# Three tile groups of an attention and two-layer kernel placed 64 bytes further on, and attention's conversions begun in other groups

## The chip, the cores and the metric

The kernel runs on one core of one Trainium2 chip. The metric is the device time of one execution in microseconds (us). Before the change the median of three executions is 1054.4 us (1048.92 to 1058.47).

## What is computed

```python
def _attn_ref(q, k, v):                       # q, k, v: (4, 12, 448, 64)
    S = q.shape[2]
    scores = np.matmul(q, k.transpose(0, 1, 3, 2)) / np.sqrt(64) - np.log(S)
    return np.matmul(1.0 / (1.0 + np.exp(-scores)), v)

def _moe_ref(x, w_in, w_out):                 # x: (1792, 768), w_in: (768, 2048), w_out: (2048, 768)
    h = x @ w_in
    return (h / (1.0 + np.exp(-h))) @ w_out

def _moe2_ref(x, w_in, w_out, a, b):          # the same sizes
    h = x @ w_in
    P = a[0] + a[1]*h + a[2]*h**2 + a[3]*h**3
    Q = 1.0 + abs(b[0])*abs(h) + abs(b[1])*h**2
    return (P / (Q + 1e-06)) @ w_out

# out = _moe2_ref(_moe_ref(heads of _attn_ref side by side, ...), ...)
```

The weights arrive as 64-bit floats and are cut to 32-bit ones on the chip.

## The kernel before, in words

**Three stages, one order.** The program fixes the order of the work by hand: each engine runs its instructions in the order in which they stand in the code. A wait on an engine holds up all that stands behind it there. Attention (L1009 to L1120) comes first, then layer 1 (its first product with `w_in1` in 16 groups by Strassen's seven products, its second with `w_out1` behind it), then layer 2.

**Operands in two parts.** For more precision each matmul operand is split into a high part (a copy on ACT) and a low part (a subtraction on DVE). A product is then three matmuls: high by high, high weights by low x, low weights by high x. Layer 1's first product (`product`, L540 to L552) issues 16 groups x 7 products x 9 = 1008 matmuls of 448 columns. Its weights are the parts `wr` and `wq`; its moving side is x in the tiles `xb` and `xa_all`. Layer 1's second product (`second`, L687 to L697) streams parts in `xa_all` against weights `woH`, `woL`. Layer 2's first product (`first2`, L756 to L772) streams x parts that lie either in the six `hx` tiles or in `xa_all`, against `woH`, `woL`, with 512 or 384 columns. The weight parts of index 0 and 1 lie in the four tiles `w0` (the profile calls them `w`).

**Attention.** The 24 pairs of heads are worked two at a time: an even pair e and an odd one o = e+1. One round of e has three groups (`quads`, L1036 to L1047). Below they are called A, B and C:

- A: steps n = 2e and 2e+1; units (e,0), (e,1), (e,2); no new pair.
- B: step 2e+2; units (o,0), (o,1); prepares pair e+2.
- C: step 2e+3; units (o,2) and (e,3), the second of which is shared by both pairs; prepares pair e+3.

A unit is `attn_QK` on PE (L351, k's parts as weights, q's parts moving, 448 columns, two halves of the array side by side), then a sigmoid on ACT (`attn_S`, L366), and one group later `attn_AV` on PE (L375). Three PSUM tiles `pair` go round. A unit takes one until its sigmoid has read it; a prepared pair's transposed k (`attn_T`, L323) takes one until the copy on ACT (L334) and the subtraction on DVE (L336) have read it. `attn_E` (L388, L391) empties `hb` on DVE in group A, before the next `attn_AV` of that round may write it. `attn_X` (L328) transposes q on DVE. From e = 6 on, each group also begins a split of layer 1's x (L408 on ACT, L413 on DVE, some subtractions L450 on POOL).

**Conversions.** `conv` (L194) cuts a 128x768 slab of 64-bit weights. It is an `Abs` on ACT that waits for the slab's load (L203), two cheap DVE operations (L204, L205), and the `rest`: two DVE operations (L208, L211). In attention it is begun at the end of the group that holds step n, if n is in `CONVS`; the rest runs in the following group, behind that group's `attn_C` (or behind `attn_E` in A); and `conv_outs` at the start of the group after that sends the result away on the SP queue (L177) and asks for the next slab (`conv_load`, L161 and L163). The first two slabs are asked for at n = 0 and n = 3. Twelve conversions are begun in attention, the others in the layers.

**Where the tiles lie.** Offsets within a partition follow from the sizes of the tiles. The left pools begin with `sb`, `ident` and five small tiles, so `xa_all` begins 32 bytes behind a multiple of 128; `xb`, `wr`, `wq` and `woH2` to `woL15` all are whole multiples of 128 behind it, and so do they. k's parts (`kst`) and two of q's three buffers (`qst`) lie in `xa_all`, also at 32. The right pools end at a fixed address; `hx`, `w0` and q's third buffer `qx` begin 96 bytes behind a multiple of 128. The slices that the matmuls take out of the tiles begin whole multiples of 128 into them.

Of the kernel before, what the change touches and what calls it, by code (L numbers as in the profile page):

```python
# [11 lines left out]
F32 = mybir.dt.float32  # L12
# [29 lines left out]
def attention_moe_moe(ctx: ExitStack, tc: tile.TileContext, q, k, v, w_in1, w_out1, w_in2, w_out2, a, b2, out):  # L42
    nc = tc.nc
    B, H, S, D = q.shape
    NT, DM = out.shape
    DFF = w_out1.shape[0]
    P = 128
# [9 lines left out]
    BK = 512  # L57
    ONE = 1.0 + 1e-6
    QKSCALE = 1.0 / math.sqrt(D)
    NEG_LOG_S = -math.log(S)  # L60
    NST = 2

    cpool = ctx.enter_context(tc.tile_pool(name="cpool", bufs=1))
    dr_p = ctx.enter_context(tc.tile_pool(name="dr", bufs=1, space=DRAM))

    def fixed(nm, n, shape, dt, pool=cpool):
        return [pool.tile(shape, dt, tag=f"{nm}{i}", name=f"{nm}{i}") for i in range(n)]

    def opened(name, side=None, space=None):
        stack = ExitStack()  # L70
        kw = {"space": space} if space is not None else {}
        if side is not None:
            kw["side"] = side
        pool = stack.enter_context(tc.tile_pool(name=name, bufs=1, reuse_waits="tile", **kw))
        ctx.push(stack)
        return pool, stack

    REST_SB = DM - S
    sizes = (10 * S, 3 * BK, *(2 * DM,) * NST, *(DM,) * 2, REST_SB)
    sb = cpool.tile([P, sum(sizes)], F32, tag="sb", name="sb")  # L80
    sb_at = [sum(sizes[:i]) for i in range(len(sizes) + 1)]
# [6 lines left out]
    xio = Ring([x_all[:, i, :] for i in range(3)])  # L88
    stage = Ring([t.bitcast(I32).rearrange("p (e t) -> p e t", t=2) for t in sb_[2 : 2 + NST]])
    bits = Ring(sb_[2 + NST : 4 + NST])  # L90
    xs = [[dr_p.tile([P, NT], F32, tag=f"xs{m}_{d}", name=f"xs{m}_{d}") for d in range(KD)] for m in range(2)]
# [79 lines left out]
    def conv_outs():  # L171
        for do in outs:
            do()
        outs.clear()
# [64 lines left out]
    ld_p = [None]  # L239
# [18 lines left out]
    def load_k(i):  # L258
        if i < NPT:
            ks[i] = ks_t[i % 4]  # L260
            load_by_key(k, ks[i], i, nc.scalar if i < 2 else nc.sync)

    def load_q(i):
        if i >= NPT:
            return
        b, hp = divmod(i, NP)
        t = qs[i] = ld_p[0].tile([P, S], F32, tag="qs", name=f"qs_{i}", bufs=3)
        for part in range(2 * D // SQ):
            j, e0 = divmod(part * SQ, D)
            (nc.scalar if i == 0 and part % 2 else nc.sync).dma_start(  # L270
                out=t[part * SQ : (part + 1) * SQ, :].rearrange("l (c d) -> l c d", d=SQ),
                in_=q[b, 2 * hp + j, :, e0 : e0 + SQ].rearrange("(c l) d -> l c d", l=SQ),
            )
# [3 lines left out]
    def mix(i):  # L277
        if i >= NPT:
            return
        t = ks.pop(i)  # L280
        u = mixed[i] = ld_p[0].tile([P, 2 * NCH * D], F32, tag="km", name=f"km_{i}", bufs=2)
        (nc.gpsimd if i else nc.vector).tensor_copy(
            u.rearrange("p (c h d) -> p h c d", c=NCH, h=2), t.rearrange("p h (c d) -> p h c d", c=NCH)
        )
# [8 lines left out]
    xa_all = xa_p.tile([P, 9 * 2 * S], F32R, tag="xa_all", name="xa_all")  # L293
# [6 lines left out]
    xk_p, xk_s = opened("xk")  # L300
    xk = fixed("xk", 2 * KD, [P, S], F32, xk_p)
    wr, wq = [], []
    K3 = 3 * 2 * BK
    kst = Ring([xa_all[:, i * 2 * BK : (i + 1) * 2 * BK].rearrange("p (j s) -> p j s", j=2) for i in range(3)])
    qst = Ring([xa_all[:, K3 + i * 2 * S : K3 + (i + 1) * 2 * S].rearrange("p (j s) -> p j s", j=2) for i in range(2)])

    hb = []
    st, at = {}, {}
# [17 lines left out]
    def attn_X(i):  # L326
        x = xq[i] = ld_p[0].tile([P, S], F32, tag="xq", name=f"xq_{i}", bufs=1)
        nc.vector.transpose(x, qs.pop(i))  # L328
# [35 lines left out]
    def attn_S(i, c, p):  # L364
        t = f2.get()
        nc.scalar.activation(t, p[:, :, :S], AF.Sigmoid, bias=nls, scale=QKSCALE)  # L366
        pairs.put(p)
        at[i, c] = t
# [42 lines left out]
    def flush():  # L411
        for src, h, lo in lows:
            nc.vector.tensor_tensor(out=lo, in0=src, in1=h.bitcast(F32), op=ALU.subtract)  # L413
        lows.clear()
# [37 lines left out]
    def operands0():  # L452
        X, W, Y, Z = (xk[n_ * HK : (n_ + 1) * HK] for n_ in range(4))
        for kk in range(HK):
            split_p(X[kk], 0, "11", kk)
            yield
            split_p(W[kk], 0, "21", kk)
            if kk == HK - 1:
                sub_p(X[0], Y[0], X[0])
            yield  # L460
        for kk in range(HK):
            x, w, y, z = X[kk], W[kk], Y[kk], Z[kk]
            split_p(x, 0, "T1", kk)
            sub_p(y, z, y)
            yield
            split_p(y, 0, "T3", kk)
            yield
            split_p(z, 0, "22", kk)
            sub_p(y, z, x)
            yield  # L470
            split_p(y, 0, "T2", kk)
            sub_p(w, w, y)
            if kk + 1 < HK:
                sub_p(X[kk + 1], Y[kk + 1], X[kk + 1])
            yield
            split_p(w, 0, "T4", kk)
            yield
# [525 lines left out]
    with tc.manual_schedule():  # L1003
# [7 lines left out]
        pairs.put(*fixed("pair", 3, [P, 2, 512], F32, ps_p))  # L1011
        ks_t.extend(fixed("ks", 4, [P, 2, NCH * D], F32, ld_p[0]))
        qst.put(ld_p[0].tile([P, 2, S], F32R, tag="qx", name="qx"))
        for i in range(2):
            load_k(i)
            load_q(i)
# [14 lines left out]
        load_q(3)  # L1031
        load_k(4)
        first_ops = operands0()
        CONVS = (3, 6, 10, 14, 18, 22, 26, 29, 33, 36, 39, 42)
        waiting = []
        def quads():  # L1036
            for e in range(0, NPT, 2):
                o, n = e + 1, 2 * e
                if e == 0:
                    yield e, (0,), [(e, 0), (e, 1)], 1  # L1040
                    yield e, (1,), [(e, 2)], 2
                    yield e, (2,), [(o, 0), (o, 1)], NPT
                    yield e, (3,), [(o, 2), (e, LAST)], 3
                else:
                    yield e, (n, n + 1), [(e, 0), (e, 1), (e, 2)], NPT
                    yield e, (n + 2,), [(o, 0), (o, 1)], e + 2
                    yield e, (n + 3,), [(o, 2), (e, LAST)], e + 3  # L1047

        for e, steps, units, new in quads():
            conv_outs()  # L1050
            flush()
            if 0 in steps:
                mix(2)
            for n in steps:
                if n % 2:
                    mix(n // 2 + 3)
            if new < NPT:
                attn_X(new)
            ready = [(u, attn_QK(*u)) for u in units]
            p = attn_T(new) if new < NPT else None  # L1060
            for u, p_ in ready:
                attn_S(*u, p_)
            for u in waiting:
                attn_AV(*u)
            waiting = units
            if steps[0] == 2 * e and e:
                attn_E(e - 2)
                attn_E(e - 1)
            if p is not None:
                attn_C(new, *p)  # L1070
            if new < NPT:
                load_q(new + 3)
            conv_rest()
            if e >= NP:
                next(first_ops, None)
            for n in steps:
                i, h = divmod(n, 2)
                if h == 0:
                    load_k(i + 5)
                at_half = n - 2 * NPT  # L1080
                if n % 4 == 1:
                    load_v(e + 2)
                    load_v(e + 3)
                if at_half == -8:
                    load_w1(0)
                    load_w1(1)
                if at_half == -5:
                    xk_s.close()
                    wr_p, wr_s = opened("wr")
                    wr.extend(fixed("wr", 4, [P, DM], F32R, wr_p))  # L1090
                    wq.extend(fixed("wq", 6, [P, HM], F32R, wr_p))
                    prep_ij(0)
                    sums_12(0)
                if at_half == -3:
                    prep_s12(0)
                if at_half == -1:
                    prep_a22(0)
                if n == 0:
                    conv_load()
                if n == 3:  # L1100
                    conv_load()
                if n == 4:
                    coefficients()
                if n == 12:
                    coefficients_abs()
                if n in CONVS:
                    conv(True)
# [8 lines left out]
        ps_s.close()  # L1116
        w0_p = ctx.enter_context(tc.tile_pool(name="w0", bufs=1, side="right", reuse_waits="tile"))
        w0 = fixed("w0", 4, [P, DM], F32R, w0_p)
        woH.extend(w0[0::2])
        woL.extend(w0[1::2])  # L1120
        kt_p, kt_s = opened("kt", side="right")
# [233 lines left out]
        for n in range(HN):  # L1355
            g, p = turn(n)
# [31 lines left out]
            if n > 3 * HF:  # L1388
                i = n - 3 * HF - 1
# [85 lines left out]
```

## Time and profile before

| | us |
|---|---|
| executions: median (lowest, highest) | 1054.4 (1048.92, 1058.47) |
| the profiled execution | 1053.23 |
| its span, first to last instruction | 1051.4 |
| PE busy | 1036.2 (99% of the span) |
| DVE, ACT, POOL busy | 773.3, 605.8, 263.8 |
| attention, until layer 1's first matmul | about 167.8 |

The time is that of the whole execution; the span is what the profile sees of it, 1.8 us less. PE counts as busy while any matmul is on its way, and matmuls overlap, so 99% doesn't mean that each streams at its best rate: the distance from one matmul's start to the next one's is what counts.

### The profile page before, as it was taken

What the parts mean: (1) busy time and instruction counts of PE and PEld (TensorE: products, weight loads), DVE (VectorE), ACT (ScalarE), POOL (GpSimd) and SP (SyncE); (2) the same over time, 40 slices, a digit from 0 to 9 for tenths busy, and PEclk for the clock granted to TensorE, in tenths of its full rate; (3) what the DMA queues carried; (4) which work ended last, traced back from release to release, by engine and by line L of the source; (5) the groups of instructions that cost most, each with busy time, mean ns of one, the idle gap of its engine ahead of it and who ended that gap; (6) DMA issues with size and microseconds to landing.
All of it is one profiled execution on the core that took longest, in us unless ns stands there. A gap on an engine that the chain in (4) does not pass through costs nothing.

```text
span 1051.4 us, 15990 instructions
## 1 busy us (share of the span) xinstructions
PE 1036.2 (99%) x5558; PEld 895.7 (85%) x5558; DVE 773.3 (74%) x1104; ACT 605.8 (58%) x911; POOL 263.8 (25%) x233
## 2 busy tenths in 40 slices
PE   8999999999999999999999999999999999999998
PEld 5555457999998988899998888888999999999998
DVE  3678885888978758686877847879898977545761
ACT  4788785556655545433343458666777857354430
POOL 4235520000000000000000046769868931300000
PEclk9999999999999999999999999999999999999999
DMA  9989895777558765799899844657678878876641
GB/s 172 234 196 202 226 263 198 264 257 244 187 200 287 253 234 201 241 316 320 295 338 351 319 166 135 236 177 233 240 255 309 291 253 298 312 228 200 210 159 52
DMA packets 184288, 251.06 MB, mean 239 GB/s; under 512 B 57360, under 2 KB 136464, under 8 KB 184208
## 3 DMA queue, kind: packets, MB, share of 16 engines
q1 hardware_dynamic: 169824, 225.48, 66.3%
q10 hardware_dynamic: 12016, 19.06, 5.6%
q0 software_dynamic: 2368, 5.51, 2.3%
q8 instruction: 43, 0.70, 0.3%
q14 instruction: 37, 0.30, 0.1%
HBM read 166.17 MB, written 83.82 MB: 238 GB/s over the span
## 4 chain that ended last, share of the span: by engine, by line
PE 75%; DVE 10%; DMA 4%; ACT 3%; POOL 3%; issue 3%; SPq 2%; ACTq 0%; DVEq 0%; POOLq 0%
PE acc L546 14%; PE hp L959 13%; PE acc L693 5%; PE acc L694 5%; PE acc L695 5%; PE hb L546 5%; PE hb L959 5%; PE hb L375 4%; PE pair L351 3%; PE hp L766 3%; PE hp L767 3%; PE hp L768 3%; POOL sb L886 2%; DMA qs<-in_q_dram 2%; PE hb L694 2%
## 5 line engine op out<-in xcount | busy, mean ns | idle before, releaser
L403 POOL TENSOR_TENSOR woL<-wif,woH 128x768 fp32r<-128x768 f32 x9 | 16.5, 1850 | 466.2 <-ACT woH L402 466.2
L203 ACT ACTIVATE sb<-sb 128x768 f32<-128x768 f32 x64 | 57.8, 904 | 61.3 <-DMA w1i<-sb 28.7
L695 PE MATMUL acc<-xa_all,woL 128*128 128x512 f32 (+1 forms) x252 | 91.9, 365 | 0.0
L693 PE MATMUL acc<-xa_all,woH 128*128 128x512 f32 (+1 forms) x252 | 91.9, 365 | 0.0
L694 PE MATMUL acc<-xa_all,woH 128*128 128x512 f32 (+1 forms) x252 | 91.9, 365 | 0.0
L366 ACT ACTIVATE sb<-pair,nls 128x896 f32<-128x896 f32 x84 | 80.2, 1007 | 16.1 <-PE pair L351 16.0
L795 POOL TENSOR_TENSOR sb<-sb 128x1024 f32<-128x1024 f32 (+1 forms) x32 | 70.1, 2191 | 38.0 <-ACT sb L792 38.0
L375 PE MATMUL hb<-sb,vs 128*64 128x448 f32 (+1 forms) x384 | 73.3, 556 | 1.6 <-DVE sb L391 1.1
L546 PE MATMUL acc<-xb,wr 128*128 128x448 f32 x315 | 68.5, 367 | 0.0
L211 DVE SCALAR_TENSOR_TENSOR sb<-sb 128x768 int32<-128x768 int32 x64 | 62.9, 984 | 2.2
L886 POOL TENSOR_TENSOR sb<-sb 128x384 f32<-128x384 f32 (+1 forms) x43 | 50.2, 1174 | 57.2 <-DMA sb<-gk 55.3
L546 PEld LDWEIGHTS acc<-xb,wr 128*128 128x128 f32 x315 | 59.1, 188 | 6.2 <-issue 0.7
L208 DVE SCALAR_TENSOR_TENSOR sb<-sb 128x768 int32<-128x768 int32 x64 | 62.5, 977 | 1.8
L766 PE MATMUL hp<-hx,woH 128*128 128x512 f32 (+1 forms) x168 | 61.6, 367 | 0.0
L767 PE MATMUL hp<-hx,woH 128*128 128x512 f32 (+1 forms) x168 | 61.6, 367 | 0.0
L768 PE MATMUL hp<-hx,woL 128*128 128x512 f32 (+1 forms) x168 | 61.6, 367 | 0.0
L766 PE MATMUL hp<-xa_all,woH 128*128 128x512 f32 (+1 forms) x168 | 60.7, 362 | 0.0
L768 PE MATMUL hp<-xa_all,woL 128*128 128x512 f32 (+1 forms) x168 | 60.7, 362 | 0.0
L767 PE MATMUL hp<-xa_all,woH 128*128 128x512 f32 (+1 forms) x168 | 60.7, 362 | 0.0
L797 DVE TENSOR_TENSOR sb<-hp,sb 128x768 f32<-128x768 f32 (+1 forms) x31 | 33.6, 1084 | 35.2 <-ACT sb L794 35.2
L351 PEld LDWEIGHTS pair<-xa_all 64*128 64x128 f32 x384 | 35.1, 190 | 24.8 <-ACT sb L366 10.4
L204 DVE TENSOR_SCALAR sb<-sb 128x768 f32<-128x768 f32 x64 | 36.0, 562 | 25.2 <-ACT sb L203 24.9
(242 smaller groups left out, 2764.5 us busy)
## 6 DMA issues: line engine op xcount, KB each, us to landing
sb<-in_moe_w_in_dram SPq DMA_DIRECT2D x32, 768.0 KB, 7.3
sb<-in_moe_w_out_dram SPq DMA_DIRECT2D x32, 768.0 KB, 6.5
gd<-sb SPq DMA_DIRECT2D x64, 224.0 KB, 3.4
wf<-w0i SPq DMA_DIRECT2D x32, 384.0 KB, 3.9
gk<-sb SPq DMA_DIRECT2D x27, 384.0 KB, 3.9
gk<-sb SPq DMA_DIRECT2D x15, 512.0 KB, 3.0
woL<-gk SPq DMA_DIRECT2D x25, 256.0 KB, 4.8
w0i<-sb SPq DMA_DIRECT2D x16, 384.0 KB, 3.1
```

The lines of the kernel that those rows point to most:

```text
L366: nc.scalar.activation(t, p[:, :, :S], AF.Sigmoid, bias=nls, scale=QKSCALE)
L375: nc.tensor.matmul(hb[i_ % 2][j * D : (j + 1) * D, :S], vs[i_][part, j, c * D : (c + 1) * D], t[part, j], start=(c == 0), stop=(c == LAST),)
L546: nc.tensor.matmul(o, w_[:, w], x[:, i_, :], start=first and kk == 0 and n_ == 0, stop=kk == HK - 1 and n_ == 2, skip_group_check=not first,)
L693: nc.tensor.matmul(o, woH[c][:, w], x[:, 0, :w_], start=(c == 0), stop=False)
L694: nc.tensor.matmul(o, woH[c][:, w], x[:, 1, :w_], start=False, stop=False)
L695: nc.tensor.matmul(o, woL[c][:, w], x[:, 0, :w_], start=False, stop=(c == KF - 1))
L766: nc.tensor.matmul(o, wh[:, w], x[:, 0, :wd_], start=first, stop=False)
L767: nc.tensor.matmul(o, wh[:, w], x[:, 1, :wd_], start=False, stop=False)
L768: nc.tensor.matmul(o, wl[:, w], x[:, 0, :wd_], start=False, stop=last)
L795: nc.gpsimd.tensor_tensor(out=q_, in0=q_, in1=a_, op=ALU.mult)
L886: nc.gpsimd.tensor_tensor(out=o, in0=i0, in1=i1, op=op)
L959: nc.tensor.matmul(o, a_, y[:, w_, :], start=kk == 0 and n_ == 0, stop=kk == HF - 1 and n_ == 2)
```

## The change

Four things, all in placement and order; no operation is added or taken away except three tiles that nothing reads or writes.

- `wr` gets a tile of 112 floats (448 bytes) ahead of it in its pool: `wr` and `wq` now begin 96 bytes behind a multiple of 128, x in `xb` and `xa_all` stays at 32.
- `w0` gets such a tile behind it. Its pool ends at the fixed right end, so `w0` and all pools to the left of it (`hx` among them) move down by 448 bytes, from 96 to 32.
- In `xa_all`, q's two buffers now stand ahead of k's three, with 112 floats between: k's parts begin at 96, q's at 32. A 64-byte tile behind `qx` moves it from 96 to 32. So all three q buffers stand at 32 and k at 96.
- `CONVS` begins conversions at steps 5, 7, 11, 13, 15, 19, 23, ... 43. Before, of twelve conversions the first fell into C, the next six into B, three into A, one into C and one into B. After, two (the first, and that at 13) fall into A and ten into C.

The unused end of `sb` gives 512 bytes for it, a multiple of 128.

```diff
+    PAD = 112
-    REST_SB = DM - S
+    REST_SB = DM - S - P
@@ the parts of k and q in xa_all
-    K3 = 3 * 2 * BK
-    kst = Ring([xa_all[:, i * 2 * BK : (i + 1) * 2 * BK].rearrange("p (j s) -> p j s", j=2) for i in range(3)])
-    qst = Ring([xa_all[:, K3 + i * 2 * S : K3 + (i + 1) * 2 * S].rearrange("p (j s) -> p j s", j=2) for i in range(2)])
+    Q2 = 2 * 2 * S
+    qst = Ring([xa_all[:, i * 2 * S : (i + 1) * 2 * S].rearrange("p (j s) -> p j s", j=2) for i in range(2)])
+    k_at = [Q2 + PAD + i * 2 * BK for i in range(3)]
+    kst = Ring([xa_all[:, i : i + 2 * BK].rearrange("p (j s) -> p j s", j=2) for i in k_at])
@@ attention
         qst.put(ld_p[0].tile([P, 2, S], F32R, tag="qx", name="qx"))
+        ld_p[0].tile([P, 16], F32, tag="qxpad", name="qxpad")
-        CONVS = (3, 6, 10, 14, 18, 22, 26, 29, 33, 36, 39, 42)
+        CONVS = (5, 7, 11, 13, 15, 19, 23, 27, 31, 35, 39, 43)
@@ layer 1's weight parts
                     wr_p, wr_s = opened("wr")
+                    wr_p.tile([P, PAD], F32, tag="wrpad", name="wrpad")
                     wr.extend(fixed("wr", 4, [P, DM], F32R, wr_p))
@@ behind attention
         w0 = fixed("w0", 4, [P, DM], F32R, w0_p)
+        w0_p.tile([P, PAD], F32, tag="w0pad", name="w0pad")
```

## Rows read from the trace of the kernel before

**Rows 1.** The page's first part: busy time and share of the span.

```profile
PE 1036.2 (99%) x5558; PEld 895.7 (85%) x5558; DVE 773.3 (74%) x1104; ACT 605.8 (58%) x911; POOL 263.8 (25%) x233
```

**Rows 2.** Chain of waits, 17 to 28 us: start, us, what.

```profile
18.32 7.38 DMA sb<-in_moe_w_in_dram
...
26.52 1.00 ACT sb L366
```

**Rows 3.** Timeline, PE, 27 to 47 us: start, us, what, count [idle before <-releaser].

```profile
27.57 2.39 PE L351 MATMUL pair<-xa_all 64*128 64x448 f32 x12 [2.85 <-ACT sb L366]
...
33.61 0.89 PE L351 MATMUL pair<-xa_all 64*128 64x448 f32 x6
...
41.72 1.48 PE L351 MATMUL pair<-qx,xa_all 64*128 64x448 f32 x12
...
46.12 0.87 PE L351 MATMUL pair<-qx,xa_all 64*128 64x448 f32 x6
```

**Rows 4.** Windows: stretch, us; busy (count) per engine; PE's granted clock, DMA share, GB/s.

```profile
27.50:31.50 4.00, 3.93 (x18) 2.33 (x20) 3.75 (x6) 4.00 (x6) 0.37 (x1) 0.58 1.10 193
```

**Rows 5.** Timeline, all engines, 17 to 38 us: the second slab's load and its `Abs`.

```profile
27.97 0.48 SPq L161 DMA_DIRECT2D sb<-in_moe_w_in_dram  x1
...
34.91 0.90 ACT L203 ACTIVATE sb<-sb 128x768 f32<-128x768 f32 x1 [2.81 <-DMA sb<-in_moe_w_in_dram]
```

**Rows 6.** Waits of PE, 32 to 168 us: total us, times, longest us.

```profile
PE pair L351 <- DVE xa_all L336: 1.3, 3, 0.5
PE hb L375 <- DVE sb L391: 1.1, 1, 1.1
PE hb L375 <- DVE xk L388: 0.5, 1, 0.5
```

**Rows 7.** Timeline, all engines, 152 to 159 us: the last conversion on DVE, and `attn_E`.

```profile
152.26 0.56 DVE L205 TENSOR_SCALAR sb<-sb 128x768 int32<-128x768 int32 x1
...
156.06 0.96 DVE L211 SCALAR_TENSOR_TENSOR sb<-sb 128x768 int32<-128x768 int32 x1
...
158.86 1.15 DVE L391 COPY sb<-hb 128x448 f32<-128x448 f32 x2
```

**Rows 8.** Timeline, all engines, 84 to 131 us: the same operation while POOL works.

```profile
89.93 1.78 DVE L211 SCALAR_TENSOR_TENSOR sb<-sb 128x768 int32<-128x768 int32 x1
```

**Rows 9.** Groups by line and shape, PE: out<-moving,weights; count | busy us, mean ns | idle.

```profile
L546 PE MATMUL acc<-xb,wr 128*128 128x448 f32 x315 | 68.5, 367 | 0.0
...
L766 PE MATMUL hp<-hx,woH 128*128 128x512 f32 x84 | 33.2, 396 | 0.0
...
L766 PE MATMUL hp<-xa_all,woH 128*128 128x512 f32 x84 | 32.7, 389 | 0.0
...
L766 PE MATMUL hp<-hx,woH 128*128 128x384 f32 x84 | 28.4, 338 | 0.0
...
L766 PE MATMUL hp<-xa_all,woH 128*128 128x384 f32 x84 | 28.1, 334 | 0.0
...
L694 PE MATMUL acc<-xa_all,w 128*128 128x512 f32 x20 | 7.9, 393 | 0.0
```

**Rows 10.** Timeline, PE, layer 1 near 300 us.

```profile
302.91 2.02 PE L546 MATMUL acc<-xa_all,wq 128*128 128x448 f32 x9
304.77 1.40 PE L546 MATMUL hb<-xb,wq 128*128 128x448 f32 x6
```

**Rows 11.** Timeline, PE, layer 1 near 180 us.

```profile
180.68 1.98 PE L546 MATMUL acc<-xb,wq 128*128 128x448 f32 x9
182.50 1.79 PE L546 MATMUL hb<-xb,wr 128*128 128x448 f32 x8
```

**Rows 12.** Windows, layer 1's first product alone (L546): the same columns, without DVE, ACT, POOL.

```profile
167.80:215.00 47.20, 47.19 (x233) 43.75 (x234) 1.00 0.64 216
```

**Rows 13.** Timeline, PE, attention: three units with q in `xa_all`, then in `qx`.

```profile
87.92 2.09 PE L351 MATMUL pair<-xa_all 64*128 64x448 f32 x18
...
101.03 2.08 PE L351 MATMUL pair<-qx,xa_all 64*128 64x448 f32 x18
```

## Prediction

> **What bounds the kernel now.** I read the page first: PE is busy in 99% of the span, the next engine in 74% [rows 1]. So a change can help in two ways only: it takes out a wait of PE, or it brings the starts of matmuls closer together. Then I read PE's waits and the chain of waits in attention, for the first; and the durations by shape and the distances of starts in the layers, for the second.
>
> In attention there is one large wait. The chain shows the first slab of `w_in` underway until 25.7 us; right behind it come the `Abs` and the sigmoid that PE waits for [rows 2]. PE stood still for 2.85 us before 27.57 [rows 3]. Behind that wait it was slow as well: in the next 4 us its granted clock was 0.58 [rows 4], that is, it fell from the 2.4 to the 1.2 GHz level for about 3.4 of these 4 us ((1 - 0.58) / 0.5 x 4), having been idle. From 32 us to the end of attention the waits of PE come to 2.9 us, all for DVE [rows 6].
>
> In the layers PE hardly waits, but the same shape takes different times. In layer 2 a 512-column matmul takes 396 ns with x in `hx` and 389 ns with x in `xa_all`; 384 columns take 338 and 334 ns [rows 9]. The weights `woH` are the same, the clock is full. What differs is that `hx` lies at 96 behind a multiple of 128 and `xa_all`, like the weights, at 32. Durations include a tail that overlaps the next matmul; where matmuls follow each other without a gap, a difference in duration is one in the distance of starts. Layer 1's 448 columns should lie halfway between 334 and 389, at 361.5 ns; they take 367 [rows 9]. Near 300 us nine of them take 304.77 - 302.91 = 1.86 us, 206.7 ns each [rows 10]; near 180 us 182.50 - 180.68 = 1.82 us, 202.2 ns [rows 11]. The window up to 215 us agrees: 47.2 us / 233 = 202.6 ns [rows 12]. So one and the same placement ran at two rates, and offset is not all that matters.
>
> **The change, part by part.** The time is worked out against the profiled execution, 1053.2 us, which lies 1.2 us under the median of the three.
>
> *First conversion, from step 3 (C) to step 5 (A of e = 2): -4.1 us.* The `Abs` now stands behind A's three sigmoids. Those are ready by about 24.5 us, so ACT waits for a slab that lands at 25.7 with nothing due ahead of it; group B can start when A's matmuls end. That gives back the 2.85 us and the slow stretch: this B took 33.61 - 27.57 = 6.04 us, the B of e = 4 took 46.12 - 41.72 = 4.40 us [rows 3], so 1.6 us more; 4.5 together. Queued behind the `Abs` are B's two sigmoids on ACT, and on DVE the conversion's cheap operations and pair 4's transpose. They start near 26.6, B's units are computed about then, and three `pair` tiles are just enough. The second conversion moves from step 6 to 7. Its slab is asked for at 27.97 and lands at 34.9 [rows 5], which the change doesn't move; but PE is some 4.5 us further on, so this `Abs` now holds ACT until 35.8 while A of e = 4 (from about 33.4) wants its sigmoids. Three pairs let PE run on to about 37; I charge 0.4 us. Bounds: -4.6 (no charge) and -2.0 (PE loses the whole wait of 2.81 less 0.3 [rows 5] again).
>
> *Conversions at 11, 13 and 15: +0.8 us.* Three stand close together here. The rest of one and the cheap part of the next meet in A of e = 6, and the slab for 15 is asked for later than before, since it needs the buffer of 11's. I take one rest less one cheap part, 1.9 - 1.1 [rows 7], as what doesn't fit. Bounds 0 and 3 (the whole wait for a slab, 2.81 [rows 5]).
>
> *The others, from B and A to C: -1.4 us.* A rest is two operations, 2 x 0.96 = 1.9 us [rows 7], or up to 2 x 1.78 = 3.6 where POOL works beside it [rows 8]; the cheap part is 2 x 0.56 = 1.1 us [rows 7]. In B or C it stands in the way of the subtraction that frees a `pair` tile; from C it runs in A, where DVE has no pair to prepare, behind `attn_E`. Then B prepares its pair with DVE about 1 us behind, and has about 1.9 us for it before the tile is wanted. I take most of the waits for `xa_all` and `xk`, 1.3 + 0.5 [rows 6], less a fifth for stretched ones. Bounds 0 and -1.8.
>
> *Last one, from 42 to 43: -0.8 us.* Before, its rest (to 157.02) ran ahead of `attn_E` at 158.86 [rows 7], and PE waited 1.1 us for that [rows 6]. After, the rest comes behind it but its cheap part ahead: 1.9 - 1.1 = 0.8. Bounds 0 and -1.1.
>
> *The order on the SP queue: 0.* The store of a finished slab moves from the head of A or C to the head of B, with the next slab's load, ahead of B's q loads. Those wait for pair e+2's transpose anyhow, which stands behind the same rest on DVE. They are needed one and a half rounds later. If that cover is gone, q lands late and a transpose waits: in the +0.8's bound.
>
> *k and q opposite in attention: 0.* q in `qx` (96, weights 32) and in `xa_all` (32 and 32) both occur now: 18 matmuls take 2.08 and 2.09 us [rows 13]. The new pairing is 32 against 96. Bounds: 288 pairs by 2.7 ns less or 4 more: -0.8 and +1.2.
>
> *Layer 2's `hx` to 32: -2.5 us.* Three lines of 84 matmuls: 252 x 7 ns at 512 columns, 252 x 4 at 384 [rows 9]: 1.8 + 1.0 = 2.8. I take 2.5, since durations are rounded. Bounds -2.0 and -3.0.
>
> *`w0` to 32: -0.3 us.* About 108 matmuls of 512 columns pair weights at 96 with x at 32, at 393 against 389 ns at worst [rows 9].
>
> *Layer 1's weights to 96, x at 32: -3.5 us.* This exact pairing exists only at 512 columns: 393 instead of 389 in the worst of three lines, +2 to +3 on the mean. So I expect about 2.2 ns above the floor. The floor at 448 columns is 206.7 less the 6 ns that 367 lies above 361.5, about 200.2: so 202.4. Of 1008 matmuls 233 ran at 202.6 and 775 at 206.7 [rows 10, 12]: 775 x 4.3 = 3.3, and 0.1 for the others. Bounds: the floor, 775 x 6.5 + 233 x 2.4 = -5.6; and as far above it as `hx` was at 512 columns (7 ns, 207.2): 775 x 0.5 + 233 x 4.6 = +1.5.
>
> The Trainium skill (TensorE: Matmul & The Clock Gate, "Step-by-step: what each phase is for") says that moving operand and weights are read through two ports, and that loading the next weights doesn't take read bandwidth from the running matmul. By that no offset would cost anything, the last three terms would be zero, and the sum -5.5. The rows of `hx` against `xa_all` speak against it.
>
> Sum: -4.1 + 0.8 - 1.4 - 0.8 - 2.5 - 0.3 - 3.5 = -11.8; 1053.2 - 11.8 = **1041.4 us**.
>
> **The rivals.**
>
> *Layer 1 doesn't gain.* The pairing 32 against 96 does at 448 columns what 96 against 32 does at 512. For it: the rates of [rows 10] and [rows 11] show that the placement alone doesn't fix the rate. Against it: the 393 of [rows 9]. The time: all at 206.7 instead of the mixture is 233 x 4.1 = 1.0 more, so 1041.4 + 3.5 + 1.0 = 1045.9.
>
> *Offsets do nothing.* What looks like placement is the neighbourhood. For it: two rates with one placement. Against it: `hx` and `xa_all` alternate in layer 2, by turns, and each keeps its duration. Attention's terms alone: 1053.2 - 5.5 = 1047.7. By the rule of the Trainium skill named above it would go so.
>
> *Slower: the rest in A blocks pair e+2.* DVE runs `attn_E`, the rest, then transpose and subtraction for B's pair; ACT's copy of q waits for the transpose, and C's sigmoids stand behind the copy. I count about 0.9 us of slack. Where a rest is stretched beyond that (by up to 3.6 - 1.9 = 1.7 us [rows 7, 8]), ACT's order makes PE wait for the `pair` tile, and what is late is late again in C. If PE loses a whole stretched rest in each of ten rounds, that is +36: 1077. With an unstretched one, +19, it is 1060, already slower than before. Against it: DVE has 26% of its time left [rows 1], and B has no conversion of its own now.
>
> **How the numbers follow.** My forecast has 0.62, with a range of its own from 1036 to 1046: the terms' nearer bounds. Layer 1 without gain has 0.16, offsets without effect 0.14, the slower case 0.06; 0.02 is left. The range for all reaches from 1034 (all best bounds sum to -17.2, so 1036, and 2 us for the spread of executions) to 1050 (offsets without effect, and most of the bound of +3 on top); it leaves out the slower case and tails, some 0.15. A measurement of this kernel can tell about 1% from no change: 10.5 us, so 1043.9 and 1064.9 about the median. Faster by over 1%: four fifths of the forecast's 0.62 and a third of layer 1's rival, 0.55. Slower by over 1%: 0.05. Within: 0.40.
>
> **What would show it.** The first `Abs` waits without PE waiting behind it, and no stretch of low clock near 28 us; attention ends at about 162 us instead of 167.8; waits of PE for DVE there fall from 2.9 to about 1 us. `hx` and `xa_all` both at 389 and 334 ns. Layer 1's nine matmuls at 1.82 us instead of 1.86. I am wrong if PE waits for `pair` again and again behind ACT or DVE, or if layer 1's duration stays at 367 ns or more.

## The result, and the profile after

| us | before | after |
|---|---|---|
| median (lowest to highest), 14 executions each | 1052.22 (1048.63 to 1058.47) | 1040.96 (1039.21 to 1048.31) |
| the profiled execution | 1053.23 | 1048.31 |
| its span | 1051.4 | 1046.5 |
| attention, until layer 1's first matmul | 167.81 | 167.82 |

The ratio is 0.9902, with a 95% interval of 0.9886 to 0.9918: 0.98% faster. The forecast was 1041.4 us with a range of 1034 to 1050, so the median lies 0.4 us from it. A change of 1% lies inside the interval, so "faster by over 1%" and "within 1%" can't be told apart. The profiled execution of the changed kernel is the slowest of its 14, 7.4 us above their median. The larger part of that comes from one wait in attention, which is the most useful thing in this trace; a smaller part comes from two waits at the end of layer 1's first product.

First the places where the kernel before was slow. The timeline of PE of the changed kernel (start, us, engine, line, operation, out<-in, count, [idle before <-releaser]), at rounds e = 2 and e = 4. Lines of the code stand 1 or 2 further on than before (the QK matmul of L351 is now L353, the `Abs` of L203 is L204, layer 1's matmul of L546 is L548, `hx`'s of L766 is L768).

```profile
24.57 1.48 PE L353 MATMUL pair<-xa_all 64*128 64x448 f32 x12
...
37.50 1.77 PE L353 MATMUL pair<-qx,xa_all 64*128 64x448 f32 x12 [0.36 <-ACT sb L368]
```

And the window behind the old stall (us; busy time and count of PE, PEld, DVE, ACT, POOL; granted clock; DMA share; GB/s).

```profile
27.50:31.50 4.00, 4.00 (x32) 2.34 (x28) 3.40 (x6) 2.74 (x5) 0.61 (x1) 1.00 1.15 186
```

Group B of e = 2 now begins at 24.57 without a wait, where it began at 27.57 after one of 2.85 us [rows 3]. The granted clock there is 1.00 instead of 0.58 [rows 4]: the 2.4 GHz level all through. B of e = 4 begins at 37.50 instead of 41.72.

So at 37.5 us the changed kernel is 4.2 us ahead, and yet at the end of attention it is level. PE's waits from 32 to 168 us (engine, line, waited for: us in total, times, longest) show where that went.

```profile
PE pair L353 <- ACT sb L368: 5.1, 3, 4.3
PE pair L353 <- DVE xa_all L338: 0.5, 1, 0.5
PE pair L325 <- DVE xa_all L338: 0.5, 1, 0.5
```

In the kernel before, the waits for DVE were 3.3 us in this window, not the 2.9 of [rows 6]: the same view has a fourth line.

```profile
PE pair L323 <- DVE xa_all L336: 0.4, 2, 0.2
```

They fell from 3.3 us to 1.0. But there is a new wait of 4.3 us, for a sigmoid. The chain of waits from 59 to 72 us (start, us, what) says what lies behind it:

```profile
59.53 7.47 DMA sb<-in_moe_w_in_dram
...
67.08 0.04 ACT sb L204
...
67.86 1.00 ACT sb L368
...
68.92 2.39 PE pair L353 x12
```

It is the same picture as before at 18 to 28 us [rows 2], with the fifth slab in place of the first: a slab of `w_in` underway until 67.0, the `Abs` that waits for it, behind the `Abs` the sigmoids, and PE behind those. The timeline of all engines adds who was late:

```profile
52.65 0.96 DVE L212 SCALAR_TENSOR_TENSOR sb<-sb 128x768 int32<-128x768 int32 x1
...
52.85 2.11 SPq L271 DMA_DIRECT2D qs<-in_q_dram  x4
...
55.05 3.74 SPq L253 DMA_DIRECT2D ks<-in_k_dram  x2
...
58.89 0.54 SPq L178 DMA_DIRECT2D w0i<-sb  x1
...
59.53 0.39 SPq L162 DMA_DIRECT2D sb<-in_moe_w_in_dram  x1
...
67.08 0.89 ACT L204 ACTIVATE sb<-sb 128x768 f32<-128x768 f32 x1 [4.70 <-DMA sb<-in_moe_w_in_dram]
...
68.92 2.39 PE L353 MATMUL pair<-xa_all 64*128 64x448 f32 x12 [4.29 <-ACT sb L368]
```

This is the conversion begun at step 15. There are two slabs in flight at a time: the one for 15 can be asked for only when the conversion begun at step 11 has stored its result. That one's rest ends on DVE at 53.6, in group A of e = 6; its store stands on SP behind q's and k's loads, goes out at 58.89, and the load follows at 59.53. One group later its `Abs` stands on ACT ahead of the sigmoids of A of e = 8 and holds them for 4.70 us. PE waits 4.29 us, and the clock falls behind the wait as it did at 28 us before:

```profile
68.90:72.90 4.00, 3.98 (x18) 2.33 (x20) 3.97 (x7) 4.00 (x6) 0.42 (x1) 0.57 1.00 320
```

The other part of the slow execution lies near 368 us, where layer 1's second product begins. Waits of PE from 320 to 400 us:

```profile
PE hb L695 <- ACT sb L623: 1.8, 1, 1.8
PE acc L548 <- ACT sb L623: 0.3, 1, 0.3
```

In the second measurement of this kernel (the first experiment below) this window has no wait.

In the layers, the groups by line and shape of the changed kernel (out<-moving,weights; count | busy us, mean ns of one | idle), beside [rows 9]:

```profile
L548 PE MATMUL acc<-xb,wr 128*128 128x448 f32 x315 | 66.9, 362 | 0.0
...
L768 PE MATMUL hp<-hx,woH 128*128 128x512 f32 x84 | 32.7, 389 | 0.0
L768 PE MATMUL hp<-xa_all,woH 128*128 128x512 f32 x84 | 32.7, 389 | 0.0
...
L768 PE MATMUL hp<-hx,woH 128*128 128x384 f32 x84 | 28.1, 334 | 0.0
```

`hx` and `xa_all` take the same now, and a matmul of layer 1's largest group 362 ns instead of 367. Its starts, from the timeline of PE near 300 us:

```profile
299.95 1.96 PE L548 MATMUL acc<-xa_all,wq 128*128 128x448 f32 x9
301.75 1.96 PE L548 MATMUL hb<-xb,wq 128*128 128x448 f32 x9
```

Nine take 301.75 - 299.95 = 1.80 us, 200.0 ns each, where it was 206.7 [rows 10] or 202.2 [rows 11]. That is the floor that the prediction had worked out (200.2), not the 202.4 that it expected.

### The profile page after: what moved, and what is told of

Its sections match the earlier page's. It is cut to its first block, busy times and chain, and to the rows that moved or that the text cites. A ratio compares the mean times of both kernels' runs of the same rounds, so it can differ in the third digit from the quotient of the medians.

```text
span 1046.5 us, 15991 instructions
## 1 busy us (share of the span) xinstructions
PE 1028.7 (98%) x5558; PEld 894.0 (85%) x5558; DVE 776.7 (74%) x1104; ACT 605.1 (58%) x911; POOL 262.9 (25%) x233
## 4 chain that ended last, share of the span: by engine, by line
PE 69%; DVE 16%; DMA 5%; ACT 5%; issue 3%; POOL 1%; SPq 1%; ACTq 0%; DVEq 0%
PE hp L961 14%; PE acc L548 12%; PE acc L696 5%; PE acc L695 5%; PE acc L697 5%; PE pair L353 5%; PE hb L377 5%; PE hb L961 5%; PE hb L548 4%; DVE sb L801 3%; DVE sb L799 2%; DVE sb L814 2%; DVE hb L815 2%; DMA sb<-in_moe_w_in_dram 2%; ACT sb L796 2%
## 5 line engine op out<-in xcount | busy, mean ns | idle before, releaser
L204 ACT ACTIVATE sb<-sb 128x768 f32<-128x768 f32 x64 | 57.9, 904 | 60.7 <-DMA w1i<-sb 28.1
L368 ACT ACTIVATE sb<-pair,nls 128x896 f32<-128x896 f32 x84 | 80.2, 1008 | 12.8 <-PE pair L353 12.6
L548 PE MATMUL acc<-xb,wr 128*128 128x448 f32 x315 | 66.9, 362 | 0.0
L548 PEld LDWEIGHTS acc<-xb,wr 128*128 128x128 f32 x315 | 59.0, 187 | 4.6 <-issue 0.7
L768 PE MATMUL hp<-xa_all,woH 128*128 128x512 f32 (+1 forms) x168 | 60.8, 362 | 0.0
L768 PE MATMUL hp<-hx,woH 128*128 128x512 f32 (+1 forms) x168 | 60.8, 362 | 0.0
L353 PEld LDWEIGHTS pair<-xa_all 64*128 64x128 f32 x384 | 35.1, 192 | 25.8 <-ACT sb L368 11.3
L794 ACT ACTIVATE sb<-sb,absb 128x1024 f32<-128x1024 f32 (+1 forms) x32 | 36.4, 1139 | 33.5 <-DVE hb L815 33.2
L353 PE MATMUL pair<-xa_all 64*128 64x448 f32 x384 | 49.6, 390 | 5.5 <-ACT sb L368 4.7
```

Source lines behind the costliest of these rows:

```text
L353: nc.tensor.matmul(p[:, j, :S], K[rows[j], a_, c * P : (c + 1) * P], Q[rows[j], b_, :], start=(n == 0), stop=(n == len(turns) - 1),)
L548: nc.tensor.matmul(o, w_[:, w], x[:, i_, :], start=first and kk == 0 and n_ == 0, stop=kk == HK - 1 and n_ == 2, skip_group_check=not first,)
L768: nc.tensor.matmul(o, wh[:, w], x[:, 0, :wd_], start=first, stop=False)
```

## Experiments

Three questions were open. Does the wait at step 15 return in other executions, and which edit makes it? What are the two halves, order and placement, worth by themselves? And what about a placement counts? Medians are given as "kernel (kernel before beside it)", ratios with their 95% intervals.

**The changed kernel once more.** No edit.

> The changed kernel once more, unaltered. The profiled execution of it took 1048.3 us, the slowest of 14 whose median is 1041.0; PE waited 4.3 us for a pair tile behind the conversion of step 15, whose slab landed at 67.0 us, and its clock fell for 3.4 us behind that. Theory 'late slab': most executions don't lose that much there, so another profile of an execution near 1041 shows the wait before 69 us well under 4 us, no stretch of low clock there, and attention over by 161 to 163 us instead of 167.8; layer 1's matmuls again near 200 us / 1000 in distance (362 ns in duration). Rival 'always': the wait at 64 us stands in every execution (4 us or more), attention ends near 167.8 and the median's gain comes from somewhere else in the layers.

1042.19 us (1051.97), ratio 0.9906 (0.9889 to 0.9922). In its profiled execution, 1042.36 us, the wait is there again, shorter. Waits of PE, 55 to 70 us, and the `Abs` with the matmuls that follow it in the timeline:

```profile
PE pair L353 <- ACT sb L368: 2.4, 1, 2.4
```

```profile
55.37 1.51 SPq L162 DMA_DIRECT2D sb<-in_moe_w_in_dram  x1
...
63.30 0.89 ACT L204 ACTIVATE sb<-sb 128x768 f32<-128x768 f32 x1 [2.85 <-DMA sb<-in_moe_w_in_dram]
...
65.14 1.19 PE L353 MATMUL pair<-xa_all 64*128 64x448 f32 x6 [2.43 <-ACT sb L368]
```

The slab for 15 was asked for at 55.37 instead of 59.53, so the `Abs` could begin at 63.30 instead of 67.08. Attention ended at 164.57, later than the 161 to 163 expected, and the clock fell behind this wait too, which was not expected. Window of this kernel:

```profile
65.00:69.00 4.00, 3.87 (x18) 2.40 (x20) 3.97 (x7) 4.00 (x6) 0.80 (x2) 0.57 0.99 245
```

The 5.9 us between the spans of the two profiled executions are 3.3 us in attention (167.82 against 164.57) and 2.8 us from there to layer 2's first matmul (437.2 against 434.4), less 0.1 in layer 2.

Three more kernels below have the same order of conversions: the new order alone, everything 32 bytes less, and `hx` another 128 bytes away. Their slabs for step 15 were asked for at 54.91, 53.76 and 55.57, PE waited there 0.5 us at most for ACT and 0.8 for DVE, and attention ended at 162.93, 161.38 and 162.35. So the place is crowded in every execution, but only two of the five lost much there. The latest request went with the largest wait; between 53.8 and 55.6 us the time of the request alone doesn't order the waits.

**The new order alone.** The kernel before with

```diff
-        CONVS = (3, 6, 10, 14, 18, 22, 26, 29, 33, 36, 39, 42)
+        CONVS = (5, 7, 11, 13, 15, 19, 23, 27, 31, 35, 39, 43)
```

> The kernel before with the new list of steps alone; all tiles where they were. Theory of the prediction: attention alone gains 5.5 us, so 1046.7 us beside a before of 1052.2; layer 1 at 367 ns, hx at 396 and 338 ns as before. Rival 'late slab costs it all': the wait for the slab of step 15 eats the gain in most executions, 1050 to 1053. Rival 'offsets do nothing': this kernel takes as long as the whole change, 1041.

1047.90 us (1051.97), ratio 0.9963 (0.9945 to 0.998): 4.1 us by the medians, where the prediction's attention terms come to 5.5, inside the interval (2.1 to 5.8). Attention ended at 162.93; in this execution the slab for 15 was asked for at 54.91 and PE lost only 0.8 us there, for DVE. `hx` stayed at 396 and 338 ns, layer 1 at 367.

**The new placement alone.** The changed kernel with the old `CONVS`, the diff above the other way round.

> The changed kernel with the old list of steps: placement alone. Theory of the prediction: -3.5 (layer 1) - 2.5 (hx) - 0.3 (w0) = -6.3, 1045.9 us beside 1052.2. If layer 1 gives what the profile after shows (205.7 to 200.0 ns for 1008 matmuls, -5.7): -8.5, 1043.7. The wait of 2.85 us near 27 us and the low clock behind it stand as before. Rival 'offsets do nothing': 1052.

1047.04 us (1051.97), ratio 0.9951 (0.9934 to 0.9969): 4.9 us by the medians, less than the 6.3 of the prediction, which is still inside the interval (3.3 to 6.9), and than the 8.5 worked out from the first trace, which is not. The first stall is back, as it was before. Timeline of PE (the view ends at 28 us, so its count does too) and window of this kernel:

```profile
26.76 1.64 PE L353 MATMUL pair<-xa_all 64*128 64x448 f32 x8 [2.60 <-ACT sb L368]
```

```profile
27.50:31.50 4.00, 4.00 (x18) 2.13 (x18) 3.60 (x7) 3.78 (x6) 0.61 (x1) 0.58 1.17 207
```

So the stall belongs to the order and the layers' gain to the placement, and neither needs the other: 4.1 and 4.9, 9.0 together, against 9.8 for the changed kernel in the same set.

**Step 13 taken out of the crowd.** The changed kernel with the conversion of step 13 moved to the end:

```diff
-        CONVS = (5, 7, 11, 13, 15, 19, 23, 27, 31, 35, 39, 43)
+        CONVS = (5, 7, 11, 15, 19, 23, 27, 31, 35, 39, 43, 45)
```

> The changed kernel with the conversion of step 13 moved to step 45, so that every conversion up to 43 is a whole round from the next. Theory 'three close together': the slab for step 15 is then asked for before the rest of another conversion holds DVE, its wait goes, no execution loses 4 us near 64 us; median 1 to 2 us under the changed kernel's 1041, and the spread (1039 to 1048) shrinks to about 2 us. The late conversion may cost up to 1 us at the end of attention. Rival: slabs are late because the DMA queues are full, whatever stands beside them; then the wait stays and the time is the same as the changed kernel's.

1038.75 us (1051.97), ratio 0.9879 (0.9861 to 0.9897). Its four executions lie between 1037.97 and 1040.13, all under the 1040.18 that is the lowest of the changed kernel in the same set; of the fourteen of the first set, five lie under 1040.13. The waits of PE from 32 to 161 us are one line:

```profile
PE pair L325 <- DVE xa_all L338: 1.5, 3, 0.6
```

And the timeline of all engines of this kernel shows the `Abs` of step 15 without a wait, and group B of e = 8 behind it without one:

```profile
58.85 0.91 ACT L204 ACTIVATE sb<-sb 128x768 f32<-128x768 f32 x1
...
62.45 1.48 PE L353 MATMUL pair<-xa_all 64*128 64x448 f32 x12
```

B of e = 8 begins at 62.45, against 65.14 and 68.92. Its slab now needs the buffer of step 7's conversion, a whole round earlier. Attention ended at 160.78. With the load asked for a round earlier the wait is gone, which shows its cause: three conversions at 11, 13 and 15 with two slabs in flight. Whether the fuller DVE at that place adds to it was not separated. By the medians this version is 2.2 us under the first measurement of the changed kernel and 3.4 us under the one beside it; with four executions the intervals of the ratios still touch (0.9861 to 0.9897 against 0.9889 to 0.9922).

**Layer 1's weights alone.** The kernel before with

```diff
+    PAD = 112
-    REST_SB = DM - S
+    REST_SB = DM - S - P
+                    wr_p.tile([P, PAD], F32, tag="wrpad", name="wrpad")
```

> The kernel before with layer 1's weight parts alone moved from 32 to 96 bytes behind a multiple of 128. Theory 'pairing': layer 1's matmuls at 362 ns, 200.0 ns apart instead of 204.7 to 205.7, so 1008 x 5.2 = -5.2 us and 1046.8 us beside 1052.0; attention and layer 2 as before (hx at 396 and 338 ns). My prediction's own term was -3.5: 1048.5. Rival 'layer 1 gains only together with the other placements': 1051 to 1053, at 367 ns.

1047.77 us (1052.81), ratio 0.996 (0.9943 to 0.9977): 5.0 us by the medians. The mean distance of starts in layer 1, worked out from all starts in the trace with gaps above 250 ns left out, was 200.0 ns; `hx` stayed at 396 and 338 ns.

**`w0` and `hx` alone.** The kernel before with `PAD` and `REST_SB` as above and

```diff
+        w0_p.tile([P, PAD], F32, tag="w0pad", name="w0pad")
```

> The kernel before with w0, and with it hx, alone moved from 96 to 32. Theory 'pairing': hx at 389 and 334 ns like xa_all, -2.5 to -3.0 us for layer 2's first product and -0.3 for w0, 1049 us beside 1052.0; layer 1's first product as before at 367 ns. Rival 'offsets do nothing': 1052.

1049.68 us (1052.81), ratio 0.9963 (0.9941 to 0.9985): 3.1 us by the medians. `hx` took 389 and 334 ns. Layer 1 has its old placement here, and ran at 202.7 ns in this execution, 366 ns for one: the faster of the two rates of [rows 10, 11].

**Layer 1's weights moved by 256 bytes.** As the run with layer 1's weights alone, but

```diff
-    PAD = 112
+    PAD = 64
```

> The kernel before with layer 1's weight parts moved by 256 bytes instead of 448, so they stay at 32 behind a multiple of 128 and only the multiple changes. Theory 'the place within 128 bytes counts': layer 1 as before, 203 to 207 ns apart, 367 ns, 1052 us. Rival 'the place within 512 bytes counts', or 'any move does it': layer 1 changes, at 200 ns and 1047 us, or above 207 ns.

1052.56 us (1052.81), ratio 0.9998 (0.9977 to 1.0019): nothing. The group of layer 1 in this kernel:

```profile
L547 PE MATMUL acc<-xb,wr 128*128 128x448 f32 x315 | 67.7, 366 | 0.0
```

A tile ahead of the weights does not help as such; a move that is a multiple of 256 changes nothing.

**Everything 32 bytes less.** The changed kernel with all tiles at 0 and 64 behind a multiple of 128 instead of 32 and 96, each kept as it stands to the other:

```diff
+    cpool.tile([P, 24], F32, tag="cpad", name="cpad")
-        ld_p[0].tile([P, 16], F32, tag="qxpad", name="qxpad")
+        ld_p[0].tile([P, 24], F32, tag="qxpad", name="qxpad")
-        w0_p.tile([P, PAD], F32, tag="w0pad", name="w0pad")
+        w0_p.tile([P, PAD + 8], F32, tag="w0pad", name="w0pad")
```

> The changed kernel with 32 bytes taken off every distance: x parts, hx, w0 and woH, woL at 0 behind a multiple of 128, layer 1's weights and k's parts at 64. The pairing stays the same (32 and 96 become 0 and 64). Theory 'the difference counts': every matmul keeps its distance, 200, 227 and 173 ns at 448, 512 and 384 columns, and the time stays at 1041. Rival 'a start inside 64 bytes costs': at 0 and 64 the distances fall towards 187, 213 and 160 ns, the bare columns at 2.4 GHz; each ns on some 3900 matmuls of the layers is 3.9 us, so up to 40 us less.

1044.58 us (1052.81), ratio 0.9919 (0.9893 to 0.9945). Layer 1 ran at 200.1 ns and `xa_all` as before, so the start itself, at 32 or at 0, costs nothing. But `hx` was slow again, although it stands equal to `woH` modulo 128:

```profile
L769 PE MATMUL hp<-hx,woH 128*128 128x512 f32 x84 | 33.1, 395 | 0.0
L769 PE MATMUL hp<-xa_all,woH 128*128 128x512 f32 x84 | 32.7, 389 | 0.0
```

The left pools had moved up by 96 bytes here and the right ones down by 32, so `hx` and `woH` lay 128 bytes further apart than in the changed kernel: no difference modulo 128, but one modulo 256. That had not been foreseen, and the next run put it to the test.

**`hx` another 128 bytes away.** The changed kernel with

```diff
-        w0_p.tile([P, PAD], F32, tag="w0pad", name="w0pad")
+        w0_p.tile([P, PAD + 32], F32, tag="w0pad", name="w0pad")
```

> The changed kernel with w0 and hx another 128 bytes further down, nothing else: hx stands still equal to woH modulo 128, but 128 apart modulo 256. Theory, that the place within 256 bytes counts: hx at about 395 and 338 ns as with everything 32 bytes less, 2 to 3 us more than the changed kernel, so about 1044. Rival, that only the place within 128 bytes counts and that the other run's loss came from elsewhere: hx at 389 and 334 ns, and 1041 to 1042 us.

1045.76 us (1052.45), ratio 0.9934 (0.991 to 0.9957). The groups of this kernel:

```profile
L768 PE MATMUL hp<-hx,woH 128*128 128x512 f32 x84 | 33.1, 395 | 0.0
...
L768 PE MATMUL hp<-xa_all,woH 128*128 128x512 f32 x84 | 32.7, 389 | 0.0
...
L768 PE MATMUL hp<-hx,woH 128*128 128x384 f32 x84 | 28.4, 338 | 0.0
```

395 and 338 ns, as expected of a place that counts within 256 bytes; the rule by 128 falls for this kernel. In the median it lost 3.6 to 4.8 us against the two measurements of the changed kernel, more than the 2 to 3 expected. The traces account for 3.3: layer 2's first product took 232.9 us from its first matmul to the next stage's first instead of 230.4, and its second product 207.8 instead of 207.0, since `w0` moved too and a matmul of it with `xa_all` went from 334 to 338 ns.

**k and q alone.** The kernel before with only the parts of k and q moved in attention (the fourth item of the change).

> The kernel before with only k's and q's parts in attention moved to 96 and 32 behind a multiple of 128. The prediction priced this at 0 (-0.8 to +1.2). Theory: 0, so 1052 to 1053 us as the kernel before beside it, a ratio of 1.000 within its interval, 18 matmuls of a unit at 2.08 to 2.09 us still, and layer 1 and hx as in the kernel before. Rival, that this part takes back some of what the single parts gain (their sum is about 1 us more than the whole): a ratio above 1 by some 0.1% and attention ending 1 to 2 us later.

1052.14 us (1052.45), ratio 0.9997 (0.998 to 1.0015): nothing.

## Why the prediction came out as it did

The whole was right to 0.4 us. The steps were not all right; misses of opposite sign made up for each other, so that closeness is partly luck.

The traces allow a count by stages, each averaged over the kernels that have the same order or placement there (us; number of traces):

| stage | old | new | difference | predicted |
|---|---|---|---|---|
| attention | 169.4 (6) | 163.8 (5) | -5.6 | -5.5 |
| layer 1, to layer 2's first matmul | 438.4 (5) | 435.2 (7) | -3.2 | -3.5 |
| layer 2's first product (by the place of `hx`) | 233.1 (5) | 230.4 (5) | -2.6 | -2.5 |
| layer 2's second product, to the end | 210.6 (5) | 211.3 (5) | +0.7 | 0 |

In attention the sum is right although one term is not. The place at 11, 13 and 15 cost 3.0 us on average in the traces, where 0.8 was charged; without step 13 attention ended 8.6 us before the old order's average (7.0 before the trace that the prediction used), where the other terms add up to 6.3. Where the rest of those 8.6 comes from is not shown.

*First conversion, -4.1: right in sum.* B of e = 4 begins 41.72 - 37.50 = 4.2 us earlier [rows 3], with the 0.36 us for the second slab in it that was charged at 0.4. Over all traces it begins at 41.0 to 42.0 with the old order (six) and at 36.6 to 38.2 with the new (five). The second slab's `Abs` held ACT until 36.6 (35.63 + 0.93, as the trace of after has it), where the prediction put 35.8. The division into 2.85 for the wait and 1.6 for the slow stretch is not shown: with `w0` and `hx` alone and with k and q alone the first wait was 1.39 and 1.93 us, the clock stayed at 1.00 behind it, and yet B of e = 4 began no earlier, at 41.12 and 42.03.

*Conversions at 11, 13 and 15, +0.8: the step that failed.* The prediction saw both mechanisms, that rest and cheap part meet in A of e = 6, and that the slab for 15 is asked for late, and charged the first, leaving the second as the bound of +3. It is the second that happened. Taking step 13 away is worth 2.2 to 3.4 us at the median. In the two profiled executions of the changed kernel PE waited 4.29 and 2.43 us, and behind each wait the clock was 0.57 for 4 us; attention then ended 7.0 and 3.8 us later than without step 13 (167.82 and 164.57 against 160.78). In the three other traces with this order it ended 0.6 to 2.1 us later, and on average over the five 3.0. So the upper bound was too low as well: it took one slab wait of before [rows 5] as the worst, and left out the slow stretch behind a wait, which the prediction had itself priced at 1.6 us for the first one. The prediction also should have asked when SP gets to the load: the order on the SP queue was costed at 0, with the q loads behind the store as what could be late. What was late was the store and the slab load themselves, behind q's and k's loads.

*The other conversions and the last one, -1.4 and -0.8: right in size.* The prediction read PE's waits for DVE in attention as 2.9 us [rows 6]; with the line left out there they are 3.3. They went to 1.0 in the profiled execution and 1.5 without step 13: -1.8 to -2.3 against -2.2. The wait for `attn_E` behind the last conversion is gone.

*`hx` and `w0`, -2.5 and -0.3: right in the product, with a cost behind it left out.* The durations fell to those of `xa_all`, and layer 2's first product took 230.4 instead of 233.1 us in all five traces with `hx` and `w0` at their new place. But in these five PE waits 0.4 to 1.1 us for DVE where the second product begins, and in the seven with the slower `hx` it doesn't; the second product takes 0.7 us more on average. Alone, the part measured 3.1 (1.6 to 6.2 by the ratio). The reason given, the same place behind a multiple of 128, was only half of it. The place counts within 256 bytes, and that `hx` came out on the good side of that too was luck. Had it landed 128 off, the term would have been about 0, as two runs showed.

*Layer 1's weights, -3.5: mechanism right, size too small against this trace.* Here the prediction leaned on the worst row of `w0` at 512 columns and expected 2.2 ns above the floor. The distance is the floor, 200.0 ns. (The prediction's working of that floor, 206.7 less 6, gives 200.7; the 200.2 comes out when the 5.5 ns between 367 and 361.5 are taken from 205.7, the mean of its two rates.) Against the profiled execution, with 233 matmuls at 202.6 ns and 775 at 206.7 [rows 10, 12], that is 775 x 6.7 + 233 x 2.6 = 5.8 us. But the old placement doesn't always run that way. In the five traces that have it the mean distance was 205.7 (before), 204.7 (new order alone), 203.6 (k and q alone), 202.7 (`w0` alone) and 202.7 (weights moved by 256 bytes): 203.9 on average, so 1008 x 3.9 = 3.9 us for a usual execution. Measured alone it was 5.0 by the medians, 2.4 to 6.0 by the ratio's interval. The term was worked out against an execution that was slow in this very stage; that it still came near the usual gain is luck as well.

*k and q, 0: right*, 0.3 us with an interval on both sides of zero.

The measured single parts sum to 4.1 + 5.0 + 3.1 + 0.3 = 12.5 us against 11.3 for the whole (9.8 in the second measurement). The placement parts sum to 8.4 against 4.9 for the placement as a whole. Each has an interval of some 2 us to either side, so the sums agree only at the edge of these. The stages of the table sum to 10.7, beside 11.3, and give no sign of a loss that only all parts together have. In attention the kernel before ended at 167.8 in its trace and the five others with the old order at 169.5 to 169.9; whether placement slows attention by that, or this one execution was quick there, stays open.

The rivals: "layer 1 doesn't gain" falls by the 200.0 ns. "Offsets do nothing" falls by the two parts measured alone, whose intervals both lie under 1 (0.9943 to 0.9977 and 0.9941 to 0.9985). The Trainium skill (TensorE: Matmul & The Clock Gate, "Step-by-step: what each phase is for") says that loading the next weights takes no read bandwidth from the running matmul. The prediction drew from it that no offset would cost anything, and that doesn't hold here: the rows of `hx` at 395 and 389 ns, with the same code and 128 bytes between them, differ, and the measurement decides. Whether the loading of weights is what costs the time, no run shows. "The rest in A blocks pair e+2" didn't occur: PE's waits for DVE fell. What did occur, at one place instead of ten, is its neighbour, an `Abs` that blocks the sigmoids.

## What to carry to other kernels

Where the start of matmuls sets the time, compare the same shape with operands in different tiles; a steady difference of 1 to 3% can be a matter of placement, and a pad of a few hundred bytes is worth trying, first with a control pad that should do nothing. When a sequence of loads with few buffers is moved, work out for each load when its buffer is stored, what the issuing queue still has ahead of it then, and what its consumer holds up; one crowded place can cost its wait and a slow clock behind it. When a stage gets faster, look at what waits right behind it: here 0.7 of 2.6 us were lost again. And don't take the one profiled execution for the usual one: here both kernels' profiled executions had a stage that was slower than in the other traces that have the same code there.

## What the hardware showed that was not expected

- With 512 and 384 columns, moving operand and weights equal modulo 256 bytes gave the lowest durations (389 and 334 ns), and 128 apart gave 395 and 338. A move of layer 1's weights by 256 bytes changed nothing (0.9998).
- With 448 columns it is not the same rule: equal modulo 256 ran at two steady rates, 202 to 203 or 206 to 207 ns. Some executions kept to one, others changed from one to the other ([rows 10, 11]). 64 bytes apart gave 200.0 or 200.1 ns in all traces that have it. (The pad of 448 bytes is 64 modulo 128, as the title counts, and 192 modulo 256: the weights stand 64 behind x.) No other distance was tried at 448 columns. Why equal is best for one width and not for the other, and what picks between the two rates, was not found.
- The start itself, 32 or 0 behind a multiple of 128, made no difference (`xa_all` at 389 and 334 ns either way).
